# The reciprocal row of a sliding-block attention: spread through DRAM by a store and a broadcast load, not by VectorE's transpose

## The chip, the cores and the metric

The kernel runs on one NeuronCore of a Trainium2 chip. The metric is the device time of one execution in microseconds; lower is better. Times of several runs are given by their median. PE (TensorE) multiplies matrices, DVE (VectorE), ACT (ScalarE) and POOL (GpSimd) work element by element, and SP (SyncE) issues most of the DMA transfers. Each engine runs its instructions in order, and so does SP with the transfers that it issues.

## The reference

A block of a transformer with modulation from a conditioning vector c. S = 2048 rows, D = 576, 32 query heads on 16 key/value heads of 128, a window of the last W = 512 keys for every query, and F = 4608 in the MLP. All in float32:

```python
mod = (silu(c) @ w_mod).reshape(1, 6, 1, D)
sa, ca, ga, sb, cb, gb = mod[:, 0], ..., mod[:, 5]
h = layernorm(x) * (1 + ca) + sa
q = heads(h @ wq); k, v = k_cache[:, :, -512:], v_cache[:, :, -512:]   # each kv head serves two q heads
p = softmax(q @ k.T * 128**-0.5)          # over 512 keys
x = x + ga * ((p @ v) as (S, 4096) @ wo)
h = layernorm(x) * (1 + cb) + sb
x = x + gb * (((relu(h @ W_gate)) * (h @ W_up)) @ W_down)
```

## The kernel before, in words

Products of float32 matrices are made of three products of split operands: a rounded high part (hi, type fp32r) and the rest (lo). ACT mostly makes the high part, POOL the low part by a subtraction.

The attention is cut into 128 **units** u, one query head times 512 queries each. The scores of a unit stand transposed, keys on the partitions: psS holds two tiles of 128x1024 (two key tiles each), so that the maximum and the sum over keys run across partitions. Their way back to a 128x512 tile that holds the same row on every partition is what the change is about. For the units 4 to 107 (`by_moves(u)`, from PE0 = 4 and MOVES = 108) DVE does all of it; the units outside use PE for a part of it. A unit has these steps, with their lines:

- `s_half` twice: the score matmuls on PE (six for each half), then DVE's transposing maximum (L501), which leaves blocks of 32 keys in `t5[u]`, a tile of 12 x 16 numbers per partition.
- `max_pre(u)` (L511), `sum_pre(u - 1)` (L522: a transposing sum of the unit before's k-sum, into the same tile), and `cross(u)` (moves L534 and reductions L542): afterwards plane 0 of t5 holds the maxima and plane 1 the softmax sums of unit u - 1.
- `max_bc(u)` (L571): DVE's 32x32-block transpose of plane 0, read with a broadcast, fills the tile mb (128x512).
- `exp_half` twice: DVE subtracts mb from the scores (L591, 128x1024), ACT takes the exponential (L593) and casts the high part (L577).
- `sum_inv(u - 1)` (L547, reciprocal of plane 1, 128x16), `sum_bc(u - 1)` (L552, the transpose that fills rb, 128x512), `q_lo` (L480), and `ksum_op`: DVE adds the first two key tiles (L606), POOL the other two (L609).
- `pv_half(u - 1, 1)` on PE, then `o_mul(u - 1)` (L641): DVE multiplies the unit's output by rb. `o_hi` and `o_lo` (L645 on ACT, L649 on POOL) split it later.
- `lo_half` twice: POOL's low parts of the probabilities (L600, 128x1024).

Between these steps, `run(u, k)` inserts work of other kinds by a table of due times: weights of coming heads, the modulation sums (L130 on DVE), the gating of output weights (L223 on DVE), later layers' preparations. The order of PE, DVE, ACT and POOL is written by hand (`manual_schedule`), and each runs just what the code issues; the order of the transfers on SP is set by the framework's scheduler from its own estimates.

Three kinds of transfer share SP's queue in this stretch. Weight loads (`prep5` L190 for wq, `prep_kv` L204, `prep_out` L219 for wo) bring a raw tile into the pool rp, tag "raw", that has two buffers; `split` then casts its high part on ACT and **cuts** its low part on POOL (L183), and that frees the buffer. So a weight load waits on SP until POOL has cut the tile two loads earlier. Reloads of tiles kept in DRAM have buffers of their own. And **lays** (L1459) copy W_gate and W_up within DRAM into the layout that the MLP reads: 2x128x256 floats for the large part, 8x32x128 or 9x32x128 for the rest.

rb and mb come from the pool bp, tag "bc", of three buffers.

Of the kernel before, what the change touches and what calls it, by code (L numbers as in the profile page):

```python
# [7 lines left out]
F32 = mybir.dt.float32  # L8
# [6 lines left out]
P = 128  # L15
# [19 lines left out]
def kernel(  # L35
# [13 lines left out]
    nc = tc.nc  # L49
# [10 lines left out]
    bp = ctx.enter_context(tc.tile_pool(name="bp", bufs=3))  # L60
# [7 lines left out]
    dr = ctx.enter_context(tc.tile_pool(name="dr", bufs=1, space=bass.MemoryType.DRAM))  # L68
# [396 lines left out]
    def qproj(u, lo, hi):  # L465
        g, qb, h = unit(u)
        if lo == 0:
            assert ready[qb] == "a"
            ps = psM.tile([P, 512], F32, tag="mm", name=f"qps{u}")
            qst[u] = ps, proj_ops(ps, wqs[h], hT[qb], u in (4, 6))  # L470
        for f in qst[u][1][lo:hi]:
            f()
# [10 lines left out]
    st_, t5, pt, hi_, lo_, bc, rb, ks_, pvps, done, o, bps = ({} for _ in range(12))  # L483

    def by_pe(u):
        return u < PE0 or u >= NU - PE1

    def s_half(u, h):
        g, qb, hd = unit(u)
        k = ks[g]  # L490
        t = psS.tile([P, 2, 512], F32, tag="s", name=f"s{u}_{h}")
        st_[u, h] = t
        for j in range(2):
            kt = 2 * h + j
            ps = t[:, j, :]
            nc.tensor.matmul(ps, k[:, kt, :], qhi[u], start=True, stop=False)  # L496
            nc.tensor.matmul(ps, k[:, 4 + kt, :], qhi[u], start=False, stop=False)  # L497
            nc.tensor.matmul(ps, k[:, kt, :], qlo[u], start=False, stop=True)  # L498
        if h == 0:
            t5[u] = sp.tile([P, 12, 16], F32, tag="t5", name=f"t5_{u}", bufs=1)  # L500
        nc.vector.tensor_reduce(t5[u][:, 2 * h:2 * h + 2, :].rearrange("p k b -> p (k b)"),  # L501
                                t.rearrange("p k (b j) -> p (k b) j", j=32),
                                axis=AX.X, op=ALU.max, apply_transpose=True)

    def by_moves(u):
        return PE0 <= u < MOVES

    def max_pre(u):
        m = t5[u][:, 0:4, :].rearrange("p k b -> p b k")
        if by_moves(u):  # L510
            nc.vector.tensor_reduce(t5[u][:, 4, :], m, axis=AX.X, op=ALU.max)  # L511
            return
        bps[u] = psM.tile([P, 512], F32, tag="mm", name=f"qm{u}")
        t = bps[u][:, 128:144]
        nc.vector.tensor_reduce(t, m, axis=AX.X, op=ALU.max)
        nc.vector.tensor_tensor(t5[u][:, 4:8, :], mask[:, :, None].to_broadcast([P, 4, 16]),
                                t[:, None, :].to_broadcast([P, 4, 16]), op=ALU.mult)

    def sum_pre(u):
        if u + 1 == NU:  # L520
            t5[NU] = sp.tile([P, 12, 16], F32, tag="t5", name=f"t5_{NU}", bufs=1)
        nc.vector.tensor_reduce(t5[u + 1][:, 5 if by_moves(u + 1) else 8, :],  # L522
                                ks_.pop(u).rearrange("p (b j) -> p b j", j=32),
                                axis=AX.X, op=ALU.add, apply_transpose=True)

    def spread(u):
        a, b = (0 if u < NU else 4), (5 if u else 4)
        if u == NU:
            bps[u] = psM.tile([P, 512], F32, tag="mm", name=f"qm{u}")
        nc.tensor.matmul(bps[u][:, a * 16:b * 16], quad,  # L530
                         t5[u][:, 4 + a:4 + b, :].rearrange("p a b -> p (a b)"), start=True, stop=True)
# [4 lines left out]
    def cross(u):  # L536
        t = t5[u]
        g = t[:, 4:12, :].rearrange("p (a k) b -> p a k b", k=2)
        move(t[0:64, 6:8, :], t[64:128, 4:6, :])
        move(t[0:32, 8:12, :], t[32:64, 4:8, :])  # L540
        for k, op in enumerate((ALU.max, ALU.add)):
            nc.vector.tensor_reduce(t[0:32, k, :], g[0:32, :, k, :].rearrange("p a b -> p b a"), axis=AX.X, op=op)  # L542
        move(t[32:64, 0:2, :], t[0:32, 0:2, :])
        move(t[64:128, 0:2, :], t[0:64, 0:2, :])

    def sum_inv(u):
        nc.vector.reciprocal(t5[u + 1][:, 1, :], t5[u + 1][:, 1, :] if by_moves(u + 1) else bps[u + 1][:, 64:80])  # L547

    def sum_bc(u):
        r = t5.pop(u + 1)[:, 1, :]  # L550
        rb[u] = bp.tile([P, 512], F32, tag="bc", name=f"rb{u}")
        nc.vector.transpose(rb[u].rearrange("p (b j) -> p b j", j=32),  # L552
                            r[:, :, None].to_broadcast([P, 16, 32]))

    def max_bc(u):
        r = bps[u][:, 256:272] if by_pe(u) else t5[u][:, 0, :]
        if not by_moves(u):
            nc.vector.tensor_reduce(r, bps[u][:, :64].rearrange("p (a b) -> p b a", a=4), axis=AX.X, op=ALU.max)
            if u:
                sum_inv(u - 1)  # L560
        m = bp.tile([P, 512], F32, tag="bc", name=f"mb{u}")
        if by_pe(u):
            rr = sp.tile([P, 16, 2], F32R, tag="rr", name=f"rr{u}", bufs=1)
            nc.vector.tensor_copy(rr[:, :, 0], r)
            nc.vector.tensor_sub(rr[:, :, 1], r, rr[:, :, 0].bitcast(F32))
            nc.vector.transpose(m.rearrange("p (b s t) -> p b s t", s=2, t=16),
                                rr.bitcast(F32)[:, :, :, None].to_broadcast([P, 16, 2, 16]))
            bc[u] = bp.tile([P, 512], F32R, tag="bc", name=f"mr{u}")
            nc.scalar.copy(bc[u], m)
        else:  # L570
            nc.vector.transpose(m.rearrange("p (b j) -> p b j", j=32),  # L571
                                r[:, :, None].to_broadcast([P, 16, 32]))
            bc[u] = m
# [69 lines left out]
    def o_hi(u):  # L643
        ohi[u] = op.tile([P, 512], F32R, tag="ohi", name=f"ohi{u}")
        nc.scalar.copy(ohi[u], o[u])  # L645

    def o_lo(u):
        olo[u] = op.tile([P, 512], F32R, tag="olo", name=f"olo{u}")
        nc.gpsimd.tensor_sub(olo[u], o.pop(u), ohi[u].bitcast(F32))  # L649
# [45 lines left out]
    def piece(n):  # L695
        add = wo_piece(*pieces[n][1:], seed=seeds.get(n))

        def end():
            add()
            put_seed(n + 1)  # L700

        (pend_act if n in seeds else pend).append(end)
        return n in seeds
# [723 lines left out]
    for i in range(1, first):  # L1427
        B = 80 * i
        for c, t, gap, a in (("q", 16, 5, 0), ("kv", 24, 5, 1), ("o", 44, 6, 2)):
            if parks[c] and i > a:  # L1430
                key, d, pr = parks[c].pop(0)
# [154 lines left out]
    def after(t):  # L1586
        return next(x for x in calm if x >= t)

    t = 546
    for s in ("P1", "P2", "P4", "P7", "P5", "P6", "P3"):  # L1590
        for xx in range(2):
            for fn in w_later(s, xx, (xp, "xm", 640)):
                step("w.l", t, fn)
                t = after(t + 8)
# [40 lines left out]
    def run(u, k):  # L1635
        t = 10 * u + k
        while sched and sched[-1][0] <= t:
            fn, args = sched.pop()[2:]
            fn(*args)
# [11 lines left out]
    for u in range(NU):  # L1651
        run(u, 0)
        if u > 1 and u % 2 == 0:
            o_hi(u - 2)
            o_lo(u - 2)
        s_half(u, 0)
        s_half(u, 1)
        run(u, .5)
        max_pre(u)
        if u:  # L1660
            sum_pre(u - 1)
        if by_moves(u):
            cross(u)
            max_bc(u)
        run(u, 1)
        if u + 1 < NU:
            qproj(u + 1, 0, 14)
        else:
            piece(at[10 * u + 1])
            pv_part(u - 1, False)  # L1670
        run(u, 2)
        if not by_moves(u):
            spread(u)
            max_bc(u)
        if u + 1 < NU:
            q_hi(u + 1)
        run(u, 3)
        if 10 * u + 3 in at:
            piece(at[10 * u + 3])
        if u > 1 and u % 2:  # L1680
            o_hi(u - 2)
            o_lo(u - 2)
        run(u, 4)
        if u + 1 == NU:
            pv_part(u - 1, True)
        elif u:
            pv_half(u - 1, 0)
        flush(pend_act)
        exp_half(u, 0)
        flush()  # L1690
        run(u, 5)
        exp_half(u, 1)
        if late_hi(u):
            hi_half(u, 0)
        if u:
            if by_moves(u):
                sum_inv(u - 1)
            sum_bc(u - 1)
        if u + 1 < NU:
            q_lo(u + 1)  # L1700
        ksum_op(u, 0)
        ksum_op(u, 1)
        run(u, 6)
        if 0 < u < NU - 1:
            pv_half(u - 1, 1)
        if 10 * u + 6 in at:
            piece(at[10 * u + 6])
        run(u, 7)
        if u:
            o_mul(u - 1)  # L1710
        flush()
        run(u, 8)
        hi_half(u, 1)
        flush(pend_act)
        lo_half(u, 0)
        lo_half(u, 1)
        run(u, 9)
# [56 lines left out]
```

## Time and profile before

| | us |
|---|---|
| median of 3 runs | 2856.07 (2855.35 to 2860.0) |
| span of the profiled execution | 2855.8 |
| PE busy in it | 2815.0 |
| DVE busy | 2246.8 |
| POOL busy | 2123.8 |
| ACT busy | 1476.7 |

The profile is of one execution, and spans and starts are counted from its first instruction. An engine's busy time leaves out its waits; "idle before <- releaser" in a row of the timeline is how long the engine stood still ahead of that instruction and what ended it. SPq rows are transfers as SP issues them: their duration is SP's, not the transfer's. The DMA share is the mean over the core's 16 DMA engines, so 0.13 may be two engines at work and fourteen idle. Units 4 to 107 lie between some 98 and 1311 us.

### The profile page before, as it was taken

What the parts mean: (1) busy time and instruction counts of PE and PEld (TensorE: products, weight loads), DVE (VectorE), ACT (ScalarE), POOL (GpSimd) and SP (SyncE); (2) the same over time, 40 slices, a digit from 0 to 9 for tenths busy, and PEclk for the clock granted to TensorE, in tenths of its full rate; (3) what the DMA queues carried; (4) which work ended last, traced back from release to release, by engine and by line L of the source; (5) the groups of instructions that cost most, each with busy time, mean ns of one, the idle gap of its engine ahead of it and who ended that gap; (6) DMA issues with size and microseconds to landing.
All of it is one profiled execution on the core that took longest, in us unless ns stands there. A gap on an engine that the chain in (4) does not pass through costs nothing.

```text
span 2855.8 us, 41174 instructions
## 1 busy us (share of the span) xinstructions
PE 2815.0 (99%) x15006; PEld 2449.5 (86%) x15006; DVE 2246.8 (79%) x3384; ACT 1476.7 (52%) x2105; POOL 2123.8 (74%) x1564
## 2 busy tenths in 40 slices
PE   6999999999999999999999999999999999999999
PEld 5788888888888888888888888888888888888888
DVE  7899999999889998888889756676677466666666
ACT  5766666666766666666656444444444122222221
POOL 5688888888899989877778766788777356656653
PEclk9999999999999999999999999999999999999999
DMA  4012132222232213312243456666667844444442
GB/s 163 24 45 79 65 106 85 83 82 100 95 104 94 92 62 131 105 70 80 68 155 139 150 213 229 231 240 231 234 234 261 338 165 154 155 155 159 159 154 106
DMA packets 164506, 399.57 MB, mean 140 GB/s; under 512 B 15056, under 2 KB 62160, under 8 KB 164304
## 3 DMA queue, kind: packets, MB, share of 16 engines
q1 hardware_dynamic: 132912, 284.69, 29.9%
q10 hardware_dynamic: 31392, 112.26, 10.0%
q8 instruction: 118, 1.93, 0.3%
q14 instruction: 84, 0.69, 0.1%
HBM read 271.16 MB, written 154.57 MB: 149 GB/s over the span
## 4 chain that ended last, share of the span: by engine, by line
PE 83%; DVE 6%; POOL 5%; issue 2%; ACT 2%; DMA 2%; SPq 0%; ACTq 0%; DVEq 0%; POOLq 0%
PE gu L1016 26%; PE wo L660 12%; PE qps L424 11%; PE md L660 8%; PE st_P L1118 6%; PE s L498 3%; PE s L497 3%; PE s L496 3%; PE pv L635 3%; PE pv L634 3%; PE pv L633 3%; POOL lo L600 2%; DVE t L501 1%; DVE p L591 1%; POOL wop L795 1%
## 5 line engine op out<-in xcount | busy, mean ns | idle before, releaser
L600 POOL TENSOR_TENSOR lo<-p,hi 128x1024 fp32r<-128x1024 f32 x256 | 610.6, 2406 | 1.1 <-ACT hi L577 1.1
L609 POOL TENSOR_TENSOR ks<-ks,p 128x512 f32<-128x512 f32 x256 | 351.7, 1374 | 238.7 <-DVE ks L606 135.5
L501 DVE TRANSPOSE_TENSOR_REDUCE t<-s 128x32 f32<-128x1024 f32 x256 | 313.8, 1239 | 85.9 <-PE s L498 76.6
L1016 PE MATMUL gu<-hop_B,wop 128*128 128x512 f32 x1512 | 375.0, 391 | 0.2 <-POOL wop L795 0.2
L1016 PEld LDWEIGHTS gu<-hop_B,wop 128*128 128x128 f32 x1512 | 274.9, 188 | 51.1 <-POOL wop L795 0.9
L1016 PE MATMUL gu<-hop_T,wop 128*128 128x512 f32 x1260 | 316.1, 391 | 0.0
L424 PE MATMUL qps<-hTa,wA 128*128 128x512 f32 x1288 | 312.9, 394 | 3.1 <-DVE hTa L372 1.6
L660 PE MATMUL wo<-woga,ohi 128*128 128x288 f32 x1472 | 298.8, 295 | 2.0 <-POOL woga L183 1.4
L591 DVE TENSOR_TENSOR p<-s,mb 128x1024 f32<-128x1024 f32 x246 | 290.3, 1219 | 4.2
L424 PEld LDWEIGHTS qps<-hTa,wA 128*128 128x128 f32 x1288 | 244.5, 190 | 56.6 <-DVE hTa L372 3.2
L476 ACT ACTIVATE qhi<-qps 128x512 fp32r<-128x512 f32 x128 | 76.4, 597 | 366.9 <-PE qps L424 358.4
L660 PEld LDWEIGHTS wo<-woga,ohi 128*128 128x128 f32 x1472 | 245.9, 188 | 18.8 <-POOL woga L183 3.4
L1016 PEld LDWEIGHTS gu<-hop_T,wop 128*128 128x128 f32 x1260 | 227.8, 188 | 39.0
L577 ACT CAST hi<-p 128x1024 fp32r<-128x1024 f32 x256 | 259.5, 1042 | 1.5
L660 PE MATMUL md<-wogb,hhi 128*128 128x288 f32 x1272 | 256.9, 295 | 0.4 <-DVE acc L671 0.4
L593 ACT ACTIVATE p<-p 128x1024 f32<-128x1024 f32 x246 | 249.5, 1051 | 13.7 <-DVE p L591 13.4
L671 DVE TENSOR_TENSOR acc<-md,acc 128x576 f32<-128x576 f32 x159 | 119.9, 755 | 160.4 <-PE md L660 159.8
L660 PEld LDWEIGHTS md<-wogb,hhi 128*128 128x128 f32 x1272 | 210.9, 188 | 12.6 <-DVE acc L671 1.4
L1127 DVE TENSOR_TENSOR acc<-st_P,acc 128x576 f32<-128x576 f32 x160 | 121.1, 757 | 127.9 <-PE st_P L1118 127.9
L660 PE MATMUL wo<-woga,olo 128*128 128x288 f32 x736 | 217.8, 296 | 1.3 <-POOL olo L649 1.2
L660 PE MATMUL md<-wogb,hlo 128*128 128x288 f32 x636 | 187.5, 295 | 0.0
L649 POOL TENSOR_TENSOR olo<-rb,ohi 128x512 fp32r<-128x512 f32 x128 | 167.4, 1308 | 15.2 <-ACT ohi L645 15.0
(283 smaller groups left out, 7095.3 us busy)
## 6 DMA issues: line engine op xcount, KB each, us to landing
wop<-wk_P SPq DMA_DIRECT2D x133, 640.0 KB
wk_P<-wop ACTq DMA_DIRECT2D x119, 640.0 KB
wr<-wlay SPq DMA_DIRECT2D x68, 384.0 KB
rogb<-wd SPq DMA_DIRECT2D x68, 288.0 KB
againq<-akq SPq DMA_DIRECT2D x18, 640.0 KB
rwA<-wq SPq DMA_DIRECT2D x32, 320.0 KB
wlay<-wg SPq DMA_DIRECT2D x36, 256.0 KB
roga<-wo SPq DMA_DIRECT2D x32, 288.0 KB
```

Source lines behind the costliest of these rows:

```text
L424: return [lambda i=i, a=a, b=b: nc.tensor.matmul(ps, a, b, start=(i == 0), stop=(i == n - 1)) for i, (a, b) in enumerate(ops)]
L501: nc.vector.tensor_reduce(t5[u][:, 2 * h:2 * h + 2, :].rearrange("p k b -> p (k b)"), t.rearrange("p k (b j) -> p (k b) j", j=32), axis=AX ...
L577: nc.scalar.copy(hi_[u, h], pt[u, h])
L591: nc.vector.tensor_tensor(p, t, bc[u][:, None, :].to_broadcast([P, 2, 512]), op=ALU.subtract)
L593: nc.scalar.activation(p, p, AF.Exp, bias=0.0, scale=1.0)
L600: nc.gpsimd.tensor_sub(lo_[u, h], pt[u, h], hi_[u, h].bitcast(F32))
L609: nc.gpsimd.tensor_tensor(ks_[u], ks_[u], p[:, j, :], op=ALU.add)
L649: nc.gpsimd.tensor_sub(olo[u], o.pop(u), ohi[u].bitcast(F32))
L660: nc.tensor.matmul(ps[:, half, :H2], a[:, sl], w[b][:, cs], start=(n == 0 and seed is None), stop=(n == 5), skip_group_check=seed is not None)
L1016: nc.tensor.matmul(ps, a, c, start=s not in heir(m) and i == 0 and s not in seeds_of(m), stop=i == len(ops) - 1, skip_group_check=True)
L1118: nc.tensor.matmul(ps[:, j, :H2], x[:, sl], w[:, y, :], start=n == 0 and not second, stop=n == 2, skip_group_check=True)
L1127: nc.vector.tensor_tensor(t, ps[:, :, :H2], t, op=ALU.add)
```

## The change

In the units 4 to 107 the reciprocal of the sums of unit u - 1 is taken directly behind `max_bc(u)`, ahead of the subtractions. A 32x32 transpose by DVE then turns plane 1 (with plane 2 beside it, which isn't used), so that 16 partitions hold 32 numbers each, the 512 reciprocals; SP stores them to a small DRAM tile rd, and SP loads rd back with a broadcast to all 128 partitions into rb. `sum_bc` stays for the other units. Everything else that the program computes is as it was; SP's order is set anew by the scheduler.

```diff
+    def sum_send(u):
+        t = t5.pop(u + 1)
+        q = t[0:32, 4:6, :].rearrange("p k b -> p (k b)")
+        nc.vector.transpose(q, t[0:32, 1:3, :].rearrange("p k b -> p (k b)"))
+        d = dr.tile([16, 32], F32, name=f"rd{u}")
+        nc.sync.dma_start(d, q[0:16, :])
+        rb[u] = bp.tile([P, 512], F32, tag="bc", name=f"rb{u}")
+        nc.sync.dma_start(rb[u], d.rearrange("b j -> (b j)")[None, :].to_broadcast([P, 512]))
...
         if by_moves(u):
             cross(u)
             max_bc(u)
+            if u:
+                sum_inv(u - 1)
+                sum_send(u - 1)
...
-        if u:
-            if by_moves(u):
-                sum_inv(u - 1)
+        if u and not by_moves(u):
             sum_bc(u - 1)
```

SP's queue in the units 12 to 14 before: raw weight tiles (rwA of wq, rkv of kv) and lays; "Pool" among the waits of a load is POOL's cut, the others are transfers that used the same counter.

```order
L190 DMA rwA_2396<-wq 128x640 [waits DMAHW7_49,DMAHW0_49,Pool_49]
L1459 DMA wlay_321<-wu 2x32x128
L1459 DMA wlay<-wg 2x128x256 [waits DMAHW1_49]
L1459 DMA wlay<-wg 2x128x256 [waits DMAHW2_49]
L204 DMA rkv_1_2551<-kv 128x512 [waits DMAHW5_49,DMAHW3_49,Pool_49]
L1459 DMA wlay<-wu 2x128x256 [waits DMAHW4_49]
```

The same queue after, in the units 13 and 14, whose stores and loads are of the sums of 12 and 13:

```order
L554 DMA rd_2364<-t_13_2342 16x32 [waits DMAHW1_49,DVE_49]
L204 DMA rkv_1_2584<-kv 128x512 [waits DMAHW2_49,Pool_49]
L1468 DMA wlay<-wu 2x128x256 [waits DMAHW3_49]
L556 DMA rb_2366<-rd_2364 128x512 [waits DMAHW1_49]
L1468 DMA wlay<-wu 2x128x256 [waits DMAHW5_49]
L554 DMA rd_2495<-t_14_2473 16x32 [waits DMAHW6_49,DVE_49]
L219 DMA roga_2707<-wo 128x576 [waits DMAHW7_49,Pool_49]
L1468 DMA wlay<-wg 2x128x256 [waits DMAHW0_49]
L556 DMA rb_2497<-rd_2495 128x512 [waits DMAHW6_49]
```

Each store rd waits for DVE's small transpose, and each load rb for its store; between the two now stand a weight load that waits for POOL and a lay. In POOL's order, which is unchanged, the cut that rkv_1_2584 waits for stands directly behind both lo_half of unit 13, and the one of roga_2707 directly behind the k-sum of unit 14. Over the whole program SP has 104 stores and 104 loads more. DVE's order in unit 13 before:

```order
L571 STREAM_TRANSPOSE mb_2333<-t_13_2315 128x512
L591 TENSOR_TENSOR p_0_2379<-s_0_2308,mb_2333 128x1024
L591 TENSOR_TENSOR p_1_2382<-s_1_2317,mb_2333 128x1024
L547 RECIPROCAL t_13_2315<-t_13_2315 128x16
L552 STREAM_TRANSPOSE rb_2388<-t_13_2315 128x512
L480 SCALAR_TENSOR_TENSOR qlo_2390<-qps_2335,qhi_2351 128x512
L606 TENSOR_TENSOR ks_2392<-p_0_2379 128x512
L641 TENSOR_TENSOR rb_2388<-pv_2369,rb_2388 128x512
L130 SCALAR_TENSOR_TENSOR macc_2058<-wm_1_2272,sT,macc_2058 128x576
L501 TENSOR_REDUCE t_14_2443<-s_0_2436 128x32
```

And after:

```order
L580 STREAM_TRANSPOSE mb_2360<-t_13_2342 128x512
L547 RECIPROCAL t_13_2342<-t_13_2342 128x16
L552 STREAM_TRANSPOSE t_13_2342<-t_13_2342 32x32
L600 TENSOR_TENSOR p_0_2412<-s_0_2335,mb_2360 128x1024
L600 TENSOR_TENSOR p_1_2415<-s_1_2344,mb_2360 128x1024
L480 SCALAR_TENSOR_TENSOR qlo_2420<-qps_2368,qhi_2384 128x512
L615 TENSOR_TENSOR ks_2422<-p_0_2412 128x512
L650 TENSOR_TENSOR rb_2366<-pv_2402,rb_2366 128x512
L130 SCALAR_TENSOR_TENSOR macc_2079<-wm_1_2299,sT,macc_2079 128x576
L501 TENSOR_REDUCE t_14_2473<-s_0_2466 128x32
```

The reciprocal and a small transpose moved ahead of the subtractions, the transpose that filled rb is gone, and the multiplication by rb (L641 before, L650 after) now reads what the load brings; the next unit's reduction stands behind it as before.

## The prediction

> **What bounds the kernel now.** I read the page's first part, then the busy times over the stretch of units 4 to 107, then DVE's and POOL's timeline through one unit, then the idle times of SP's queue.
>
> ```profile
> PE 2815.0 (99%) x15006; PEld 2449.5 (86%) x15006; DVE 2246.8 (79%) x3384; ACT 1476.7 (52%) x2105; POOL 2123.8 (74%) x1564
> 98.00:1311.00 1213.00, 1205.17 (x6295) 1042.43 (x6295) 1100.41 (x1872) 818.23 (x1124) 1037.78 (x638) 1.00 0.26 85
> ```
>
> The second row (length, then PE, PEld, DVE, ACT, POOL busy, granted clock, DMA share, GB/s) is the stretch that the change touches. PE is busy for 1205.17 of 1213.00 us at a clock of 1.00: at most 7.8 us can be gained here, and DVE, with 1100.41, stands close behind. A stall of DVE by more than its slack therefore becomes time. One unit on DVE (start, duration, line, out<-in, idle time before it):
>
> ```profile
> 699.66 2.61 DVE L501 TRANSPOSE_TENSOR_REDUCE t<-s 128x32 f32<-128x1024 f32 x2 [0.96 <-PE s L498]
> ...
> 704.58 0.71 DVE L571 STREAM_TRANSPOSE mb<-t 128x512 f32<-128x512 f32 x1
> 705.32 2.35 DVE L591 TENSOR_TENSOR p<-s,mb 128x1024 f32<-128x1024 f32 x2
> 707.59 0.24 DVE L547 RECIPROCAL t<-t 128x16 f32<-128x16 f32 x1
> 707.87 0.71 DVE L552 STREAM_TRANSPOSE rb<-t 128x512 f32<-128x512 f32 x1
> 708.51 0.65 DVE L480 SCALAR_TENSOR_TENSOR qlo<-qps,qhi 128x512 fp32r<-128x512 f32 x1
> ...
> 709.68 0.68 DVE L641 TENSOR_TENSOR rb<-pv,rb 128x512 f32<-128x512 f32 x1
> 711.48 2.61 DVE L501 TRANSPOSE_TENSOR_REDUCE t<-s 128x32 f32<-128x1024 f32 x2 [1.13 <-PE s L498]
> ```
>
> A unit lasts 711.48 - 699.66 = 11.82 us. Below I count from the start of its score reduction, 699.66 here: the subtractions start at 5.66, o_mul at 10.0. DVE runs in order, so whatever makes o_mul late makes the next unit's reduction late, and PE with it.
>
> POOL's pace matters because each raw weight load waits on SP until POOL has cut the tile two loads earlier (two "raw" buffers):
>
> ```profile
> 709.90 2.67 POOL L609 TENSOR_TENSOR ks<-ks,p 128x512 f32<-128x512 f32 x2 [1.74 <-DVE ks L606]
> 712.52 1.57 POOL L183 TENSOR_TENSOR wA<-rwA,wA 128x640 fp32r<-128x640 f32 x1
> 714.05 4.78 POOL L600 TENSOR_TENSOR lo<-p,hi 128x1024 fp32r<-128x1024 f32 x2
> 195.88 2.62 DVE L501 TRANSPOSE_TENSOR_REDUCE t<-s 128x32 f32<-128x1024 f32 x2
> 208.74 4.76 POOL L600 TENSOR_TENSOR lo<-p,hi 128x1024 fp32r<-128x1024 f32 x2
> 213.45 1.58 POOL L183 TENSOR_TENSOR wA<-rwA,wA 128x640 fp32r<-128x640 f32 x1
> 215.06 0.33 SPq L190 DMA_DIRECT2D rwA<-wq  x1
> SPq L190 <- POOL kv L183: 117.8, 8, 16.3
> ```
>
> A cut behind the k-sum ends at 714.09, 14.4 into its unit; one behind lo_half at 215.03, 19.1 after 195.88, and the load on SP goes out 0.03 us later. In both, POOL's work of a unit reaches into the next one. SP spends up to 16.3 us on such a wait, and today nobody stands behind it.
>
> **The change, part by part.** *DVE.* It loses the 128x512 transpose (0.71) and gains a 32x32 one, which the trace doesn't show; the nearest rows are the smallest moves:
>
> ```profile
> L534 DVE TENSOR_REDUCE t<-t 64x32 f32<-64x32 f32 (+2 forms) x416 | 77.3, 186 | 14.3
> L542 DVE TENSOR_REDUCE t<-t 32x16 f32<-32x64 f32 x208 | 45.2, 252 | 3.6
> ```
>
> I take 0.2 (bounds 0.19 and 0.25). The reciprocal and this transpose now stand ahead of the subtractions and delay them by 0.28 + 0.2, while 0.71 + 0.28 goes from behind them: 0.5 us of DVE per unit saved. PE sets the pace there, so by itself this is worth between nothing and the 7.8 us; I take 0.
>
> *The round trip with a free queue.* The store can go at 5.66 + 0.28 + 0.2 = 6.1. Neither it nor a broadcast load is in the trace. The nearest are the smallest load and its reader, and a 256 KB load of the same tile size:
>
> ```profile
> 0.72 0.39 SPq L100 DMA_DIRECT2D cT<-c  x1
> 2.37 0.21 ACT L112 ACTIVATE sT<-cT 128x5 f32<-128x5 f32 x1 [0.37 <-DMA cT<-c]
> 742.75 0.33 SPq L204 DMA_DIRECT2D rkv<-kv  x1
> 745.00:745.50 0.50, 0.50 (x6) 0.50 (x5) 0.50 (x2) 0.50 (x2) 0.13 (x1) 1.00 0.10 33
> 1.17 1.84 SPq L108 DMA_DIRECT2D acc<-x  x4
> 4.42 0.82 DVE L285 BATCH_NORM_STATS2 sta<-acc 128x6 f32<-128x288 f32 x2 [1.22 <-DMA acc<-x]
> ```
>
> The small one is in after 1.65 us; of the 256 KB one, a last 0.10 of DMA share is seen just past 745.00, 2.4 us after its issue, and I add 0.35 until a reader may go. So rb is issued at 7.8 and can be used at 10.55; o_mul ends 0.7 later, at 11.25, inside the 11.82. Cost 0, with 0.57 us to spare. The upper bound for one transfer is the first load of x, 4.42 - 1.17 = 3.25, or 1.6 more than the small one. [...]
>
> *What stands between store and load.* SP's queue is in order. Between rd and rb the changed program's order often has a weight load that waits for POOL's cut, and behind it one of the DRAM-to-DRAM re-layout copies ("lay"). What a 2x128x256 lay does to those behind it:
>
> ```profile
> 538.08 0.59 SPq L1459 DMA_DIRECT2D wlay<-wu  x1
> 545.50:546.00 0.50, 0.50 (x4) 0.42 (x3) 0.50 (x1) 0.00 (x0) 0.50 (x1) 1.00 0.03 10
> 546.00:546.50 0.50, 0.50 (x4) 0.42 (x3) 0.47 (x2) 0.00 (x0) 0.50 (x1) 1.00 0.00 0
> 272.63 0.58 SPq L1459 DMA_DIRECT2D wlay<-wu  x1
> 273.25 7.71 SPq L1459 DMA_DIRECT2D wlay<-wg  x1
> 281.06 5.19 SPq L190 DMA_DIRECT2D rwA<-wq  x1
> 286.00:286.50 0.50, 0.50 (x4) 0.42 (x3) 0.50 (x2) 0.47 (x2) 0.50 (x1) 1.00 0.13 47
> 286.50:287.00 0.50, 0.50 (x4) 0.42 (x3) 0.50 (x1) 0.50 (x2) 0.50 (x2) 1.00 0.42 95
> 288.00:288.50 0.50, 0.41 (x3) 0.20 (x2) 0.50 (x2) 0.50 (x1) 0.24 (x1) 1.00 0.34 130
> 878.78 0.80 SPq L1459 DMA_DIRECT2D wlay<-wg  x1
> 882.50:883.00 0.50, 0.50 (x4) 0.42 (x3) 0.47 (x3) 0.00 (x0) 0.50 (x2) 1.00 0.00 0
> ```
>
> A lay issued at 538.08 ends at 545.6: 7.5 us. Two of them from 272.63 keep the DMA share at 0.13, two engines of sixteen, until some 286.4, and the load queued behind them moves its bytes only after that, until 288.3. So a load behind a lay is done between 0.7 (its share of two engines alone) and 2.0 us after the lay; I take 1.5. A last "9x32x128" lay ends before 882.50, at most 3.7 after its issue, against the load's 2.75: with its 0.8 of issuing it puts rb off by 0.8 to 2.2, and I take 1.8. [...]
>
> *Sum.* POOL's phases, re-counted for a unit whose o_mul waits (subtractions end at 5.66 + 0.48 + 2.3 = 8.4, q_lo and the first k-sum on DVE at 9.7, k-sum on POOL 9.8 to 12.4, then the rows' durations): a cut behind the k-sum ends at 14.0, lo_half at 17.1, a cut behind it at 18.7. The same cut of the unit before ends at 18.7 - 11.8 = 6.9. Counted in the changed program's order, by what stands ahead of rb:
> - load gated by the cut behind lo_half of the same unit, then a big lay: 14 units. Lay issued 19.1, done 26.6, rb 28.1, o_mul 28.8: +17.0 each, 238.
> - the same load without a big lay: 7 units. rb issued 19.1, +2.75 +0.7 = 22.6: +10.8, 75.
> - load gated by the cut behind the k-sum, then a big lay: 7 units. 14.4 + 7.5 + 1.5 + 0.7 = 24.1: +12.3, 86.
> - that load without a big lay: 9 units. 14.4 + 3.45 = 17.9: +6.0, 54.
> - a load that is free, then a big lay: 7 units. 6.9 + 7.5 + 1.5 + 0.7 = 16.6: +4.8, 34.
> - the store itself behind a load gated by the unit before, so out at about 7.75 instead of 6.1: 11.25 + 1.65 = 12.9, +1.1; 10 units, 11; with a small lay besides, 1.1 + 1.8 = +2.9; 7 units, 20.
> - the other 43: 0.
>
> That is 518. Behind o_mul stands work on DVE that today lies in its wait for PE (the 1.13 above) and does not any more in a stalled unit (11 of the stalled units have the first, 6 the second):
>
> ```profile
> L130 DVE SCALAR_TENSOR_TENSOR macc<-wm,sT,macc 128x576 f32<-128x576 f32 x12 | 18.2, 1514 | 0.0
> L223 DVE TENSOR_TENSOR roga<-roga,mrow 128x576 f32<-128x576 f32 x32 | 41.1, 1287 | 0.0
> ```
>
> 11 x 1.51 + 6 x 1.29 = 24. Against it, PE runs a few us ahead during a stall, so that a clean unit behind one can take 11.25 instead of 11.82: at most 43 x 0.57 = 25, and as only some 18 of them follow a stall closely, 10. Sum: 518 + 24 - 10 = +532. The span is 2855.8, the median 2856.1: 2855.8 + 532 + 0.3 = **3388 us**. By the bounds (1.5 between 0.7 and 2.0 on 28 units: -22, +14; 1.8 on 7: -7, +3; POOL's cuts 1 us earlier or later on 37 units: 37; lead -15, +10; counts wrong by one unit in ten: 50) this case alone runs from 3260 to 3500.
>
> **Rivals.**
> 1. *The wait for POOL is there, the collision on two engines is not* (rb's parts overtake, or the lays go out earlier). Then 21 units x 10.8 + 16 x 6.0 + 31 + 24 - 10 = +368: 3224 us. For it: no broadcast load behind a lay is in the trace; against it the load of 281.06.
> 2. *The round trip is longer*: store or broadcast read takes 1.6 us more. A slow store costs 43 x (1.6 - 0.57) + 17 x 1.6 = +71; a slow read another 44 x 1.6 = 70: 3459 to 3529 us. A read of one 2 KB row by 128 partitions could do that.
> 3. *Not slower.* If the loads between rd and rb found their tiles cut before the store is ready, rb would land at 10.55 everywhere, and the 0.5 us that DVE saves could only win back PE's idle time: 2848 to 2856 us. It decides at the cut: done by 6.1 into the unit, it holds; the rows say 14 and 18.7.
> 4. *Only latency*: the queue is free, as in 3, but the trip is 1.2 us too long in every unit: 104 x (1.2 - 0.57) = +66, 2922 us. Against it the same rows.
>
> **How the numbers follow.** Chances: forecast 0.66; rival 1 0.15; rival 2 0.12; rival 3 0.04, half of it a gain; rival 4 0.03. Some 0.2% (6 us) is what a measurement here can tell from no change. So faster 0.02, same 0.02, slower 0.96. The range takes in the forecast's own range, rival 1 with some 25 us below it, and rival 2 to its end: 3200 to 3560; left out are rivals 3 and 4 and the tails.
>
> **What would show it.** In the profile after: PE's idle time in the attention stretch grows from 8 to over 500 us; DVE's o_mul waits for the DMA rb in some 50 units; SP's waits for POOL stand ahead of rb; units with a big lay last 24 to 29 us, those with a load alone 18 to 23, clean ones 11.8; the MLP keeps its time. It is wrong if rb goes out on SP before its neighbours, if lays and rb move bytes side by side, or if clean units last longer too.

## The result, and the profile after

| | before | after |
|---|---|---|
| median of 4 runs, us | 2855.71 (2854.43 to 2860.0) | 3454.56 (3449.24 to 3457.08) |
| span of the profiled execution, us | 2855.8 | 3447.2 |
| ratio of the times | | 1.2088 (95% interval 1.207 to 1.2105) |

The kernel became slower by 599 us. Its time lies 67 us above the 3388 us that were predicted, inside the range. The first part of the page after and its chain of waits, with the chain's first row before behind them:

```profile
PE 2974.2 (86%) x15006; PEld 2529.6 (73%) x15006; DVE 2158.0 (63%) x3384; ACT 1489.3 (43%) x2105; POOL 2116.7 (61%) x1564
...
PE 44%; DVE 23%; DMA 17%; POOL 8%; issue 5%; ACT 2%; SPq 1%; DVEq 0%; POOLq 0%; ACTq 0%
PE gu L1025 22%; DMA rb<-rd 13%; PE md L669 7%; DVE t L501 7%; PE st_P L1127 5%; POOL lo L609 3%; DVE p L600 3%; DMA rd<-t 3%; PE qps L424 3%; PE wo L669 2%; DVE t L534 2%; DVE mb L580 2%; POOL ks L618 2%; DVE t L522 2%; DVE t L542 1%
PE 83%; DVE 6%; POOL 5%; issue 2%; ACT 2%; DMA 2%; SPq 0%; ACTq 0%; DVEq 0%; POOLq 0%
```

By the starts of their reductions, the units 4 to 107 lie between 94.68 and 1345.72 us before (the 98 and 1311 named ahead of the prediction stop short of the last three), and between 93.99 and 1936.00 after. The busy times over them, before and after (columns: length, PE, PEld, DVE, ACT, POOL, granted clock, DMA share, GB/s):

```profile
94.68:1345.72 1251.04, 1243.21 (x6491) 1075.26 (x6490) 1132.72 (x1930) 843.87 (x1161) 1064.91 (x654) 1.00 0.25 85
93.99:1936.00 1842.01, 1405.71 (x6496) 1158.26 (x6494) 1045.78 (x1929) 857.25 (x1162) 1059.57 (x655) 0.88 0.23 73
```

PE was idle for 7.8 us in these units before, and is idle for 436 of 1842 now, at a mean clock of 0.88; its busy time grew by 162 us for the same matmuls. DVE and POOL are no busier than they were. The load of rb alone is 13% of the chain. PE's share of the chain fell from 83% to 44%. DVE's largest wait in these units says it in one row (total, times, longest), before and after:

```profile
DVE t L501 <- PE s L498: 70.2, 66, 2.2
DVE rb L650 <- DMA rb<-rd: 719.7, 94, 19.1
```

How a single wait comes about is seen in unit 12. First DVE, then SP's queue, then POOL, all in the same unit, which starts at 237.38:

```profile
237.38 2.37 DVE L501 TRANSPOSE_TENSOR_REDUCE t<-s 128x32 f32<-128x1024 f32 x2
...
242.05 0.71 DVE L580 STREAM_TRANSPOSE mb<-t 128x512 f32<-128x512 f32 x1
242.69 0.21 DVE L547 RECIPROCAL t<-t 128x16 f32<-128x16 f32 x1
242.93 0.20 DVE L552 STREAM_TRANSPOSE t<-t 32x32 f32<-32x32 f32 x1
243.06 2.30 DVE L600 TENSOR_TENSOR p<-s,mb 128x1024 f32<-128x1024 f32 x2
...
245.89 0.67 DVE L615 TENSOR_TENSOR ks<-p 128x512 f32<-128x512 f32 x1
259.40 0.69 DVE L650 TENSOR_TENSOR rb<-pv,rb 128x512 f32<-128x512 f32 x1 [12.84 <-DMA rb<-rd]
260.01 2.37 DVE L501 TRANSPOSE_TENSOR_REDUCE t<-s 128x32 f32<-128x1024 f32 x2
```

```profile
243.16 0.32 SPq L554 DMA_DIRECT2D rd<-t  x1
243.57 0.37 SPq L138 DMA_DIRECT2D wm<-wmod  x1
255.59 0.33 SPq L190 DMA_DIRECT2D rwA<-wq  x1
255.97 0.42 SPq L556 DMA_DIRECT2D rb<-rd  x1
```

```profile
246.71 2.67 POOL L618 TENSOR_TENSOR ks<-ks,p 128x512 f32<-128x512 f32 x2 [7.22 <-DVE ks L615]
249.33 4.74 POOL L609 TENSOR_TENSOR lo<-p,hi 128x1024 fp32r<-128x1024 f32 x2
254.03 1.54 POOL L183 TENSOR_TENSOR wA<-rwA,wA 128x640 fp32r<-128x640 f32 x1
```

The store goes out 5.8 us into the unit. The weight load of wq behind it waits until POOL's cut ends at 255.57, and goes out at 255.59. Only then can the load of rb follow, 12.8 us after its store, though nothing that rb needs was missing. o_mul waits 12.84 us, and the next unit's reduction stands behind it. The unit lasts 22.6 us.

In unit 13, which starts at 260.01, a big lay stands there too. SP, the DMA share (next to last column) and DVE:

```profile
277.95 0.33 SPq L204 DMA_DIRECT2D rkv<-kv  x1
278.34 0.58 SPq L1468 DMA_DIRECT2D wlay<-wu  x1
278.97 1.87 SPq L556 DMA_DIRECT2D rb<-rd  x1
280.88 0.76 SPq L1468 DMA_DIRECT2D wlay<-wu  x1
```

```profile
282.00:283.00 1.00, 0.00 (x0) 0.00 (x0) 0.00 (x0) 0.00 (x0) 0.00 (x0) 0.50 0.54 181
284.00:284.50 0.50, 0.00 (x0) 0.00 (x0) 0.00 (x0) 0.00 (x0) 0.00 (x0) 0.50 0.13 47
285.50:286.00 0.50, 0.00 (x0) 0.00 (x0) 0.00 (x0) 0.00 (x0) 0.00 (x0) 0.50 0.14 49
```

```profile
287.39 0.69 DVE L650 TENSOR_TENSOR rb<-pv,rb 128x512 f32<-128x512 f32 x1 [18.20 <-DMA rb<-rd]
```

rb is issued at 278.97, yet o_mul starts 8.4 us later, and all engines stand still. Between 281 and 283 more than two of the DMA engines work (a share of 0.54 in the first row); from then on it is some two of sixteen. A **clean trip**, one with nothing between store and load, in unit 101:

```profile
1854.10 0.32 SPq L554 DMA_DIRECT2D rd<-t  x1
1855.46 0.33 SPq L556 DMA_DIRECT2D rb<-rd  x1
1858.69 0.69 DVE L650 TENSOR_TENSOR rb<-pv,rb 128x512 f32<-128x512 f32 x1 [1.19 <-DMA rb<-rd]
```

1.36 us from store to load, 3.23 from load to use.

### The profile page after: what moved, and what is told of

The parts are those of the page before. It is cut to its first block, busy times and chain, and to the rows that moved or that the text cites. A ratio compares the mean times of both kernels' runs of the same rounds, so it can differ in the third digit from the quotient of the medians.

```text
span 3447.2 us, 41596 instructions
## 1 busy us (share of the span) xinstructions
PE 2974.2 (86%) x15006; PEld 2529.6 (73%) x15006; DVE 2158.0 (63%) x3384; ACT 1489.3 (43%) x2105; POOL 2116.7 (61%) x1564
## 4 chain that ended last, share of the span: by engine, by line
PE 44%; DVE 23%; DMA 17%; POOL 8%; issue 5%; ACT 2%; SPq 1%; DVEq 0%; POOLq 0%; ACTq 0%
PE gu L1025 22%; DMA rb<-rd 13%; PE md L669 7%; DVE t L501 7%; PE st_P L1127 5%; POOL lo L609 3%; DVE p L600 3%; DMA rd<-t 3%; PE qps L424 3%; PE wo L669 2%; DVE t L534 2%; DVE mb L580 2%; POOL ks L618 2%; DVE t L522 2%; DVE t L542 1%
## 5 line engine op out<-in xcount | busy, mean ns | idle before, releaser
L618 POOL TENSOR_TENSOR ks<-ks,p 128x512 f32<-128x512 f32 x256 | 339.8, 1327 | 563.5 <-DVE ks L615 338.1
L650 DVE TENSOR_TENSOR rb<-pv,rb 128x512 f32<-128x512 f32 x128 | 88.1, 688 | 757.2 <-DMA rb<-rd 719.7
L642 PE MATMUL pv<-hi,kv 128*128 128x512 f32 x368 | 174.6, 475 | 272.3 <-DVE rb L650 269.5
L602 ACT ACTIVATE p<-p 128x1024 f32<-128x1024 f32 x246 | 259.6, 1058 | 319.5 <-DVE p L600 316.4
L424 PE MATMUL qps<-hTa,wA 128*128 128x512 f32 x1288 | 323.2, 403 | 30.7 <-DVE rb L650 27.6
L424 PEld LDWEIGHTS qps<-hTa,wA 128*128 128x128 f32 x1288 | 253.9, 198 | 89.5 <-DVE rb L650 28.8
L501 DVE TRANSPOSE_TENSOR_REDUCE t<-s 128x32 f32<-128x1024 f32 x256 | 304.9, 1224 | 11.5 <-PE s L498 10.4
L642 PEld LDWEIGHTS pv<-hi,kv 128*128 128x128 f32 x368 | 83.0, 226 | 297.7 <-DVE rb L650 278.9
L654 ACT CAST ohi<-rb 128x512 fp32r<-128x512 f32 x128 | 79.3, 619 | 425.2 <-DVE rb L650 405.3
```

What stands on the lines that cost most here:

```text
L424: return [lambda i=i, a=a, b=b: nc.tensor.matmul(ps, a, b, start=(i == 0), stop=(i == n - 1)) for i, (a, b) in enumerate(ops)]
L602: nc.scalar.activation(p, p, AF.Exp, bias=0.0, scale=1.0)
L618: nc.gpsimd.tensor_tensor(ks_[u], ks_[u], p[:, j, :], op=ALU.add)
L642: nc.tensor.matmul(ps, v[:, kt, :], a[:, j, :], start=(kt == 0), stop=False)
```

## The experiments

Each was run beside the kernel before on the same chip (its median was 2857.6 to 2860.3 there). Where no interval is given, it is one run.

**SP's order taken from the code.** The engine SP is added to the hand-written schedule, so that the broadcast load is issued directly behind its store.

```diff
-    ctx.enter_context(tc.manual_schedule(engines={ET.PE, ET.DVE, ET.Activation, ET.Pool}))
+    ctx.enter_context(tc.manual_schedule(engines={ET.PE, ET.DVE, ET.Activation, ET.Pool, ET.SP}))
```

> The changed kernel with SP's order taken from the code as well, so that each broadcast load stands directly behind its store; loads gated by POOL's cuts and the lays stand ahead of the store or behind the load, never between. Theory (what stands between store and load is the cost): the 51 units of 16 to 29 us shrink to 11.3 to 19 us, left are 34 stores behind a load gated by the unit before (some 2.5 us each, 85) and stores that meet a lay on its two engines (some 30 units, 3 us each, 90): 3030 us, between 2900 and 3150. Rival (the round trip itself is too long): the trip is the same, so 3300 us or more.

Measured: 3017.0 us. DVE's wait for rb in this kernel:

```profile
DVE rb L650 <- DMA rb<-rd: 244.5, 96, 10.3
```

The trip, its bytes and DVE's order are the same as in the changed kernel; 437 of the 599 us went with the order of SP's queue. The edit sets the place of every transfer on SP, so the 437 are the whole order's and not the broadcast load's alone. The rival of a trip that is too long wherever it stands (3300 or more) falls.

**The same, with lays over sixteen engines.**

```diff
-             lambda ab=ab: nc.sync.dma_start(*ab))
+             lambda ab=ab: nc.sync.dma_start(*(v.rearrange("f p n -> p f n") for v in ab)))
```

> As sp_order, in the same order of transfers, but each lay is written with its 128 or 32 rows as the slowest dimension, so that it spreads over sixteen engines. Theory (the lay holds two engines of the broadcast load's sixteen): the 90 us of lays go, 2940 us, between 2870 and 2990, and the difference to sp_order is 50 to 150 us. Rival (no collision on two engines, only the queue's order counts): the same as sp_order within 20 us. Rival (round trip too long): 3300 or more.

Measured: 2956.1 us, 61 less than with lays on two engines, in the same order of transfers. The wait for rb:

```profile
DVE rb L650 <- DMA rb<-rd: 191.1, 96, 5.1
```

The longest wait falls from 10.3 to 5.1 us. So the lay on two engines does hold rb up, and rival 1 of the prediction falls. The 61 us are fewer than the 90 that were expected for the lays, and inside the 50 to 150 that were given for the difference.

**The weight loads on POOL's queue.** The three raw loads are issued by POOL, which cuts in its own order, so nothing on SP waits for a cut. The lays stay between store and load.

```diff
-            nc.sync.dma_start(st["raw"], src[k])
+            nc.gpsimd.dma_start(st["raw"], src[k])
...
-            nc.sync.dma_start(st["raw"][:, :512], kv[g, j])
+            nc.gpsimd.dma_start(st["raw"][:, :512], kv[g, j])
...
-            nc.sync.dma_start(st["raw"][:, :D], src[k])
+            nc.gpsimd.dma_start(st["raw"][:, :D], src[k])
```

> The changed kernel with the raw weight loads issued by POOL instead of SP, so that they wait for POOL's cuts in POOL's own order and not in SP's queue; the lays still stand between store and load, in 33 units a big one, in 28 a small one. Theory: no unit waits for a gated load; 33 big lays at some 5.6 us (185), 28 small ones at 1.5 (42), so 3080 us, between 3000 and 3200, units with a big lay at 16 to 20 us; POOL's issuing may add up to 100. Rival (the gate is not what costs, the lays and the trip are): 3300 or more.

Measured: 3106.0 us, 349 less than the changed kernel.

```profile
DVE rb L650 <- DMA rb<-rd: 324.0, 95, 8.8
```

No unit is over 20.3 us any more (30.0 in the changed kernel). The 33 units with a big lay between store and load lie at 15.4 to 20.3 us, 3.5 to 8.2 over the same unit of before; of the units 44 to 62, with a small lay or none, most lie within 2 us of before. This takes the gated load off SP's queue and leaves the lay, and so shows the lay's price unit by unit, 5.1 us on average against the 5.6 expected. POOL's issuing, some 0.55 us for each load in its timeline, is in these numbers too.

**The reciprocal's place alone.** The kernel before, with `sum_inv(u - 1)` directly behind `max_bc(u)`; DVE still fills rb by its transpose, and there is no transfer.

```diff
             max_bc(u)
+            if u:
+                sum_inv(u - 1)
...
         if u:
-            if by_moves(u):
-                sum_inv(u - 1)
             sum_bc(u - 1)
```

> The kernel before with one part of the change alone: the reciprocal stands ahead of the subtractions, DVE's transpose to rb stays where it was, no store, no load. Theory (DVE's order costs nothing by itself): 2856 us within 6. Rival (0.25 us on the way to the subtractions in each of 104 units counts): 2882 us.

Measured: 2853.2 us (median of 10 runs), ratio 0.998 (0.997 to 0.9989). This part costs nothing, and wins some 6 us. In the same units:

```profile
95.13:1339.50 1244.37, 1240.80 (x6493) 1075.95 (x6492) 1113.56 (x1929) 842.63 (x1159) 1065.11 (x653) 1.00 0.26 86
```

PE's idle time is 3.6 us instead of 7.8, and DVE's busy time 1114 instead of 1133. It is the one version here that is faster than both kernels.

**Store and load on ACT's queue.** Both are issued by ACT ahead of the first exponential; SP's order is then nearly that of the kernel before.

```diff
-        nc.sync.dma_start(d, q[0:16, :])
+        sent[u] = d, q
...
+    sent = {}
...
+    def sum_dma(u):
+        d, q = sent.pop(u)
+        nc.scalar.dma_start(d, q[0:16, :])
...
-        nc.sync.dma_start(rb[u], d.rearrange("b j -> (b j)")[None, :].to_broadcast([P, 512]))
+        nc.scalar.dma_start(rb[u], d.rearrange("b j -> (b j)")[None, :].to_broadcast([P, 512]))
...
         flush(pend_act)
+        if u and by_moves(u):
+            sum_dma(u - 1)
         exp_half(u, 0)
```

> The changed kernel with store and broadcast load issued by ACT, both between the cast of q and the first exponential, so that SP's queue is again as before the change; the lays keep two engines busy beside them, on another queue. Theory (standing behind SP's gated loads and lays is the cost): no unit over 17 us; rb is issued at 7.6 to 7.9 into the unit and used 3.3 later, as in the clean units, o_mul ends at 11.6 to 11.9, the first exponential is 0.5 late: 2885 us, between 2850 and 2930. Rival (the trip is too long wherever it is issued): 3200 or more. Rival (lays hold the two engines against any queue): 3000 to 3100.

Measured: 3033.2 us, ratio 1.0619 (1.0595 to 1.0643). My 2885 was wrong here, and the number lies where the rival of lays against any queue had it. Two of its trips on ACT, a clean one and one beside lays:

```profile
336.14 0.32 ACTq L560 DMA_DIRECT2D rd<-t  x1
337.54 0.34 ACTq L562 DMA_DIRECT2D rb<-rd  x1
337.98 2.01 ACT L608 ACTIVATE p<-p 128x1024 f32<-128x1024 f32 x2 [2.28 <-DMA rd<-t]
```

```profile
356.82 0.58 SPq L1474 DMA_DIRECT2D wlay<-wg  x1
357.44 2.06 SPq L1474 DMA_DIRECT2D wlay<-wu  x1
364.29 0.33 ACTq L560 DMA_DIRECT2D rd<-t  x1
368.47 0.35 ACTq L562 DMA_DIRECT2D rb<-rd  x1
368.86 2.01 ACT L608 ACTIVATE p<-p 128x1024 f32<-128x1024 f32 x2 [6.57 <-DMA rd<-t]
```

The store takes 4.2 us instead of 1.4 in these two. Over all 104 trips the median from store to load is 1.86 us, against 1.35 in the next run, whose lays use sixteen engines. And now it is the exponential that stands behind the wait, since ACT's load waits for the store and ACT runs in order:

```profile
L608 ACT ACTIVATE p<-p 128x1024 f32<-128x1024 f32 x246 | 249.2, 1053 | 378.3 <-DMA rd<-t 271.8 <-DVE qlo L480 33.7 <-DVE p L606 31.2
```

So another queue does not get past the lay. In the trip shown the delay is 2.8 us; in the lay's own queue, in unit 13 of the changed kernel, rb was used 8.4 us after its issue instead of 3.2. What the 2885 missed is how late this makes ACT: it had the first exponential 0.5 us late, and in the median of the units it starts at 8.5 us, against 6.95 in the changed kernel. How much of the 176 us over the kernel before is ACT's lateness and how much the wait for rb isn't shown.

**The same, with lays over sixteen engines** (the edit as above).

> As trip_on_actq, with each lay spread over sixteen engines, which also lets the scheduler send nearly all of them in the first units. Theory: if lays on the other queue held rb up in trip_on_actq, this is faster than it by that much, at most 50 us; if the engines share between queues, the two are within 15 us of each other, apart from what the early lays cost at the start.

Measured: 2930.4 us, 103 less than with lays on two engines, twice what I had put as the most. The scheduler also sends the lays earlier in this version, so the 103 are not the collision alone.

**Store and load that nobody reads.** The load goes to a scratch tile in DRAM, and DVE fills rb as before the change.

```diff
-        t = t5.pop(u + 1)
+        t = t5[u + 1]
...
-        rb[u] = bp.tile([P, 512], F32, tag="bc", name=f"rb{u}")
-        nc.sync.dma_start(rb[u], d.rearrange("b j -> (b j)")[None, :].to_broadcast([P, 512]))
+        rs = dr.tile([P, 512], F32, name=f"rs{u}")
+        nc.sync.dma_start(rs, d.rearrange("b j -> (b j)")[None, :].to_broadcast([P, 512]))
...
-        if u and not by_moves(u):
+        if u:
             sum_bc(u - 1)
```

> The changed kernel with store and broadcast load kept on SP, but the load goes to a scratch row in DRAM that nobody reads, and DVE fills rb by its transpose as before the change. The scheduler sets SP's order anew, so the load stands less often behind a gated one. Theory (DVE's wait for rb is the cost, not the transfers and not the delay of SP's other loads): 2870 us, between 2850 and 2920, with DVE's small transpose and some stores late for the next unit's tile as the rest. Rival (weight loads that come late behind the stores stall PE): 3000 or more.

Measured: 2865.0 us; the units 4 to 107 are 6.9 us longer than before. With DVE not waiting, the transfers and the later weight loads cost next to nothing. SP's order is not that of the changed kernel here, so this speaks for the transfers, not for that order; and the load writes to DRAM here, not into rb.

**The kernel before in the code's order of SP, with lays over sixteen engines** (both edits as above, without the change).

> The kernel before, with SP's order taken from the code and the lays spread over sixteen engines, as in sp_order_lay16 but without the change. It prices what of that run's 100 us over the kernel before is the order by the code and not the trip. Theory: some 30 us in the MLP (its stretch was 30 us longer there) and up to 30 in the attention from late weight loads: 2900 us, between 2870 and 2930. Rival (the order costs nothing, the rest is the trip): 2856 within 8.

Measured: 2880.8 us. Its units 4 to 107 take what they took before (0.8 us less), and the rest is behind them. The run is 23 us slower than the kernel before beside it (2857.6). So of the 98 us or so that sp_order_lay16 lies above before, some 23 are SP's order and the spread lays, outside these units, and 75 the change, 70 of which its units 4 to 107 show.

**The trip earlier.** sp_order_lay16 with reciprocal, small transpose and store ahead of `max_bc`.

```diff
...
-        t = t5.pop(u + 1)
+        t = t5[u + 1]
...
             cross(u)
-            max_bc(u)
             if u:
                 sum_inv(u - 1)
                 sum_send(u - 1)
+            max_bc(u)
```

> sp_order_lay16 with the reciprocal, the small transpose and so the store ahead of max_bc's transpose instead of behind it: store and load go out 0.7 us earlier in the unit, the subtractions start where they did. Theory (of sp_order_lay16's 70 us in the units 4 to 107 most is the trip's own length, as o_mul waits for rb there by a few tenths of a us): 0.3 to 0.6 us less per unit, 2910 us, between 2890 and 2930. Rival (those 70 us come from late weight loads and transfers in the store's way, not from the length of the trip): 2956 within 10.

Measured: 2916.7 us, ratio 1.0198 (1.0181 to 1.0215), 39 less than sp_order_lay16. Its units 4 to 107 are 37.8 us longer than before instead of 70.1, and DVE's wait for rb goes from 191.1 to the row below. The store goes out 0.5 us earlier (5.27 into the unit instead of 5.79, medians), not 0.7, and the subtractions start 0.1 later (5.81 instead of 5.70).

```profile
DVE rb L650 <- DMA rb<-rd: 133.5, 93, 5.3
```

So even with the queue free the trip isn't hidden: the earlier start is paid back at 0.3 us per unit (32 us over 104 units). What the 38 us that are left consist of isn't shown.

## Why the prediction was right, by its steps

The mechanism held: a load that waits for POOL, in front of rb in SP's queue, and a lay on two engines. The mean lengthening of the units of each kind, from the starts of their reductions (L501) in the two traces:

| what stands ahead of rb, by the forecast's count | units | forecast each | measured each | measured sum |
|---|---|---|---|---|
| load gated by lo_half's cut, big lay | 14 | 17.0 | 16.5 | 230 |
| the same load, no big lay | 7 | 10.8 | 11.3 | 79 |
| load gated by the k-sum's cut, big lay | 7 | 12.3 | 12.3 | 86 |
| that load, no big lay | 9 | 6.0 | 7.4 | 66 |
| free load, big lay | 7 | 4.8 | 5.6 | 39 |
| store late, small lay | 7 | 2.9 | 3.1 | 22 |
| store late, no lay | 10 | 1.1 | 1.8 | 18 |
| the other 43 | 43 | 0 | 1.2 | 50 |

They add up to 591, and the spans differ by 591.4. In the forecast's column the first seven rows were 518, to which 24 of work behind o_mul were added and 10 of PE's lead taken away; the measured column holds both already. That the seven rows then agree to some 2 us (540 against 542) is luck in part: single rows are off by up to 12, in both directions.

- **POOL's phases** were right within 1 us in nearly all units: the cut behind lo_half ended 18.2 into unit 12, against 18.7, and the loads that wait for it went out at 17.8 to 18.5, in unit 40 at 19.8; those that wait for the cut behind the k-sum went out at 13.5 to 13.6, against 14.0, in unit 25 at 15.6.
- **The lay's collision**: rb was used 9.05 us after the lay's issue in unit 13 (287.39 - 278.34), against 7.5 + 1.5. In the 21 units with a gated load and a big lay, rb was used 7.8 to 9.1 us after its own issue; in the seven where the load waits for lo_half's cut and no big lay follows, 3.3 to 4.1. The runs with lays over sixteen engines bear out that the lay's two engines cost this time.
- **DVE's part**: the small transpose takes 0.20, as assumed. From the start of mb's transpose to the subtractions it is 1.01 us instead of 0.74, so the two operations delay them by 0.27 and not by the 0.48 that I had added up: the rows overlap by 0.07 with mb's transpose ahead and by 0.07 with the subtractions behind. The store goes out at 5.8 instead of 6.1.
- **The mis-sized term is "the other 43: 0".** They hold 50 of the 59 us by which the sum was short. Unit 4 (5.1) had a gated load that the count had missed; in the units 51, 59, 67, 74 and 76 (25.8 together) the store itself stood late in the queue and went out at 6.7 to 9.6 us; in unit 106 (1.5) DVE's small transpose was already late; the other 36 have 17.7, 0.5 each. The step "rb is issued at 7.8 and can be used at 10.55" took 2.75 us for the load by a plain load of the same tile, 0.35 of which no row had shown. The clean trip shows 3.23, and in the units from 73 on the time from the load's issue to o_mul's start, where o_mul waits for it, is 3.1 to 5.8 us, 3.4 in the median. With the earlier store (1.36 instead of 1.65) the median's end is much the same as forecast, but 0.57 us to spare was too little for loads that vary by more than that. The run with the earlier trip shows that the trip's length costs time even with the queue free: 0.5 us earlier took away 32 of the 70 us that were left with the queue in the code's order and the lays spread. That is rival 4's mechanism, as an addition to the forecast's case and not in its place. Its +66 us beside the 70 of sp_order_lay16 is chance: it had each unit late by 0.63, and there the middle eight tenths of the units changed by -0.6 to +2.3.
- **PE's lead** of -10 is seen in single units (7, 55, 63 and 77 take 10.8 to 11.4 us, against 11.8 before), but not in the sum over the 43.
- **Rival 3** (hidden, no slower) falls by each of the gated units. **Rival 2** isn't seen in its size of 1.6 us: the store is quicker than the row I had used, the load 0.5 us slower in the clean trip and 0.7 in the median named above.
- **The signs** that the prediction named came out in part. SP's waits for POOL stand ahead of rb. Units with a gated load and a big lay last 23.3 to 30.0 us, those with a gated load and no big lay 17.9 to 24.0. Outside these units the time is the same (1605.2 us, 1604.8 before). But PE's idle time grew to 436 us and not to over 500, because PE's busy time grew too, by 162; o_mul waits for rb in 94 units and not in some 50; and the clean units do last longer, which the prediction had called a sign of being wrong. The last two show the same flaw, the slack of 0.57 us.

DVE did become freer: 1046 us of busy time where there were 1133, 0.84 us per unit. The edit's terms had 0.5, which the transposes alone give (74.1 us of the one that is gone, against 104 x 0.20); the rest lies in somewhat shorter rows of other operations and isn't explained. None of it could be worth more than the 7.8 us for which PE stood idle.

## What to carry to other kernels

Before a value that an in-order engine waits for is sent through a DMA queue, read what that queue has between the two transfers: a load that waits for a slow engine's buffer costs its whole wait, once somebody stands behind it. The order of the queue here comes from the scheduler's estimates, not from the program's text, and taking it from the text was worth 437 of 599 us. A copy that covers only two DMA engines held up the transfers beside it: the broadcast load behind it in its own queue until its end, and a store on another queue by less. Turning the copy's rows outermost took 61 us away with the order of transfers unchanged.

## What the runs showed of the hardware that I had not expected

- The clock that PE is granted falls where it stands still: in unit 13 PE's last matmul ended at 275.96, the clock was 1.00 until 279.2 and 0.50 from 279.4 on; over the units 4 to 107 it was 0.88, against 1.00 before. The pv matmuls, the first to run after many of the waits, are longer by the profile (mean 475 ns against 390). Their group before, and after:

```profile
L633 PE MATMUL pv<-hi,kv 128*128 128x512 f32 x368 | 143.5, 390 | 2.8 <-DVE rr L565 2.8
```

```profile
L642 PE MATMUL pv<-hi,kv 128*128 128x512 f32 x368 | 174.6, 475 | 272.3 <-DVE rb L650 269.5 <-DVE rr L574 2.8
```

The Trainium skill ("TensorE: Matmul & The Clock Gate", Part 1) says that the clock is halved after an idle window of some 3.4 us; the 0.50, some 3.4 us after that matmul's end, agrees. How much of the 591 us lies in this clock was not measured by itself; the forecast's rows have no term for it.

- A store of 2 KB to DRAM was ready for the next transfer after 1.36 us in the clean trip (1.34 in the median of sp_order_lay16), sooner than the small load that stood for it (1.65).
- A broadcast load of a 2 KB row to 128x512 was never used sooner than 3.1 us after its issue where DVE waited for it.
- Two lays issued on SP 7 us ahead delayed a 2 KB store on ACT's queue by 2.8 us in the trip shown.
